# A new written order for the first twelve head pairs of a Longformer-attention and MLP kernel, with casting value loads and small transfers of the global value rows

## The chip, the core and the metric

The kernel runs on one core of a Trainium2 chip. A core has a matrix engine (TensorE, PE in the profile, with its weight loads as PEld), a vector engine (DVE), a scalar engine (ACT), a general engine (POOL) and a queue engine (SP). They run side by side, each through its own list of instructions in order, and wait for one another by semaphores. Transfers run on 16 shared DMA engines. Those issued by SP and ACT appear in the profile as the hardware queue, those issued by POOL as the software queue. TensorE writes its results to PSUM, where this kernel lays out eight banks of 128 x 512 fp32: three with the tag "s", two "h", one "o" and the two of `pv`.

The metric is the device time of one execution in microseconds, as the median of several runs. The profile is one execution recorded by the hardware profiler, and all times inside a run are read from it.

## What is computed

Attention over 8 batches of 8 heads (576 positions, 64 wide), with a band of 32 positions to each side and 8 global positions, and behind it an MLP over all 4608 tokens:

```python
scores = scale * np.matmul(q, k.transpose(0, 1, 3, 2))
mask = np.abs(pos[:, None] - pos[None, :]) <= window
mask = mask | is_global[:, None] | is_global[None, :]
scores = np.where(mask, scores, -1000000000.0)
...
attn = attn / (np.sum(attn, axis=-1, keepdims=True) + 1e-09)
return np.matmul(attn, v).astype(np.float32)
...
x = np.ascontiguousarray(attn_out.transpose(0, 2, 1, 3)).reshape(B * S, H * D)
h = x @ w_in
g = h * np.cos(h)
return (g @ w_out).astype(np.float32)
```

Inputs and output are fp32, `w_in` is 512 x 2048 and `w_out` 2048 x 512. The kernel computes in fp16 with fp32 sums.

## The kernel before

**Units of work.** Heads go in pairs, 32 of them (`pr`), four to a batch; two pairs are a half (`s`), which is also the unit in which k, q and v are loaded. A pair passes through these steps, each of which is one letter in a written order:

- `k` and `q` (`local_k`, `local_q`, lines 598 and 609): for pairs 0 to 9, TensorE turns the naturally laid-out rows (`turned`, line 588, 16 small transposes into one PSUM bank with the tag "h"), and ACT copies the bank to the buffers `kw` and `qb`. For pairs under `PK` = 4, 16 more small matmuls (`pick_globals`, line 307) pick the global columns out of the same rows; the other pairs get them from gathered rows through POOL copies (`g`, line 575). From pair 10 on the turning is done by DMA transposes, and DVE copies.
- `s` (`scores5`, line 621): ten matmuls `st` into three banks "s" and the one bank "o", four exponentials on ACT, three masked products `pm` on DVE.
- `p` (`values5`, line 641): 20 matmuls into `pv`, of which there is one buffer only, then on DVE the denominators and the product `xn` (line 666).
- `x` (`turn_x5`, line 670): five transposes into an "s" bank and DVE copies into `xT`, the input of the MLP. For the last pair of a batch eight POOL copies set the global columns.
- `n` (line 814): a square and sum of `xn` on ACT for a check of the value range.

Pairs 10 to 31 use a form with eleven blocks instead of five (lines 692 to 752).

**The MLP** is cut into units too. `1` is one block of `h` and its activation: four matmuls `ph` (line 762) for 512 tokens and 128 hidden columns, the cosine on ACT (line 768) and the product `g` on DVE (line 769). `2` is four of the 16 matmuls `po` (line 800) of one block of 128 output rows. A `1` for a block of tokens can only stand behind the batches that it covers (`ready`), and a `2` behind the `1`s that it needs. Cosine and exponential lie in different activation tables, so that each change from one to the other reloads a table (1283 ns in the profile).

**The order** is written by hand in strings of steps, and every engine executes its own instructions in that order. Behind a prologue (13 matmuls on ones, constants, masks, the first two turnings) stands `FRONT`: pairs 0 to 9 with no MLP unit before the step behind `x7`, in a rhythm of scores, turnings of the pair after, `x` and `p` of the pairs before, with 18 filling matmuls (`f`). Then `MID` has 26 of the units `1` and eight `2`, `FIFTH` has pairs 10 and 11 with two `1` and eight `2`, and from half 6 on `SIXTH` and then `ORDER` repeat: two pairs, eight `1` and eight `2` each. Behind the last pair the rest of the MLP runs alone.

**Loads.** POOL's queue brings k and q of a half by casting loads (`L`, line 279), the weights (`W` four times for `w_in`, `O` for `w_out`), and from half 5 on whole halves of v, k and q as fp16 into DRAM (`K`, line 268 to 272). For halves 0 to 4 the values come in fp32 by five transfers each on SP's queue (`M`, line 373), into a buffer that two halves share in turn, and a POOL cast (`C`, line 402) writes them as fp16 into the buffer `vw`, which `values5` reads. The eight global value rows of a half are then summed out of it by ten small matmuls and two ACT copies (`y`, line 404). From pair 10 on SP transposes k and q (`B`, line 284) and loads `vw` from DRAM, with the global rows `vg` copied in by two small transfers per pair (line 414). `V` and `U` are one-element POOL copies that hold back the `K` behind them until pair 10's q is there and pair 10's `xn` is done.

Of the kernel before, what the change touches and what calls it, by code (L numbers as in the profile page):

```python
# [9 lines left out]
FP32 = mybir.dt.float32  # L10
# [9 lines left out]
P = 128  # L20
NP = H // 2
# [7 lines left out]
PK = 4  # L29
# [18 lines left out]
ORDER = "sa 2 2 2 2 sz pa 1 1 2 xa pz G 1 1 2 xz n 1 1 2 kc qc 1 kd qd 2 1"  # L48
# [5 lines left out]
SIXTH = "sa 2 2 2 2 sz pa 1 1 2 xa pz G 1 1 2 xz n 1 1 D0 2 kc qc D1 1 kd qd D2 2 1"  # L54
# [150 lines left out]
def kernel(  # L205
# [44 lines left out]
    NN = 3  # L250
# [3 lines left out]
    qn = [keep.tile([QP, 2 * 2, RW, D], FP16, name=f"qn{i}") for i in range(2)]  # L254
    w_out16 = const.tile([P, NF, DM], FP16)
    kn.append(w_out16[0:KP, 0:4].rearrange("p h (r d) -> p h r d", d=D))
    qn.append(w_out16[0:QP, 4:8].rearrange("p h (r d) -> p h r d", d=D))
# [17 lines left out]
    def load_qk(s, hs=(0, 4)):  # L275

        base = (s * 4 + hs[0]) * S * D
        for src, dst in ((k, kn[s % NN][KPAD : KPAD + S // RW]), (q, qn[s % NN][0 : S // RW])):
            nc.gpsimd.dma_start(dst[:, hs[0] : hs[1]].rearrange("x h r d -> x h (r d)"),
                                dview(src, base, (RW * D, S // RW), (S * D, hs[1] - hs[0]), (1, RW * D)))  # L280
# [25 lines left out]

    def pick_globals(pr, t, src, ones, n, to):
# [5 lines left out]
        nc.scalar.copy(to, view(t, (0, to.shape[1]), (1, G)))  # L313
# [46 lines left out]
    vn32 = [work.tile([P, 4 * 2, 512], FP32, tag="g", name="vn32") for _ in range(2)]  # L360

    def vn_of(s):
        i = s if s < 4 else 2
        return view(vn32[i // 2][:, 4 * (i % 2)], (4 * D, NK5), (1, 4 * D))

    def load_vn(s, t0=0, t1=NK5):

        rows = vn_of(s)
        for t in range(t0, t1):
# [3 lines left out]
            nc.sync.dma_start(rows[p0 : p0 + n, t].rearrange("p (h d) -> p h d", h=4),  # L373
                              dview(v, (s * 4 * S + lo) * D, (D, n), (S * D, 4), (1, D)))

    def next_values(s):

        nc.vector.memset(vn_of(s)[0:64, 0], 0.0)
        load_vn(s)

    def clear_rows(s):

        nc.gpsimd.memset(vn_of(s)[0:G, 1:], 0.0)
# [11 lines left out]
    def vn16(s):  # L395
        return view(vw[s % NV], (4 * (D + 1), NK5), (D + 1, 4), (1, D + 1))

    def cast_vn(s):
        if s > 1:
            nc.gpsimd.tensor_copy(gate, pm_of[max(pm_of)][0:1, 2 * CN - 1 : 2 * CN])  # L400
        old, new = vn_of(s).rearrange("p t (h d) -> p t h d", h=4), vn16(s)
        nc.gpsimd.tensor_copy(new[:, :, :, 0:D], old)

    def value_rows(s, part):

        hs = slice(2 * part, 2 * part + 2)
# [493 lines left out]
    with tc.manual_schedule():  # L900
# [24 lines left out]
        for s in range(1, 4):  # L925
            clear_rows(s)
# [162 lines left out]
```

## Time and profile before

| | |
|---|---|
| median of 3 runs | 353.98 us (353.82 to 356.26) |
| profiled execution, its span | 353.2 us |
| PE busy | 332.5 us (94%) |
| DVE busy | 250.1 us (71%) |
| ACT busy | 245.9 us (70%) |
| POOL busy | 108.5 us (31%) |
| moved by DMA | 44.58 MB, mean 126 GB/s |
| chain that ended last | PE 73%, ACT 8%, DVE 5%, DMA 5% |

The profiled execution has no time of its own beside its span, so that the span stands for it: 353.2 us, 0.8 us under the median of the runs.

A row of a timeline gives the start in us, the busy time, the engine, the source line, the operation with what it writes and reads, and the count; in square brackets stands how long the engine was idle before it and what ended that. Instructions overlap in the engine's pipeline, so the cost of a group in a dense stretch is the distance from its start to the start of the next row rather than its busy time. A row of the stretch table gives the stretch, its length, the busy time and count for PE, PEld, DVE, ACT and POOL in this order, the granted TensorE clock (1.00 is full), the DMA share and GB/s.

### The profile page before, as it was taken

The page shows a single profiled execution, that of the slowest core. Times are in us where ns is not written, and L with a number is a line of the kernel's source. Part 1 is how long each engine was busy: PE and PEld are TensorE (multiplying, and loading weights), DVE is VectorE, ACT ScalarE, POOL GpSimd, SP SyncE. Part 2 cuts the span into 40 slices and gives each one's busy share as a digit, 9 for nine tenths or more (in the row PEclk, how much of TensorE's full clock was granted, in tenths as well). Part 3 has the DMA queues.
Part 4 walks back from the last instruction along what each step waited for, and adds up shares of the span by engine and source line. Part 5 has one row for each costly group of instructions (what it writes and reads, how often), then busy time and mean ns, then how long its engine had stood idle before and what let it go on. Part 6 is the DMA issues. An engine that isn't in the chain of part 4 may idle for free.

```text
span 353.2 us, 8389 instructions
## 1 busy us (share of the span) xinstructions
PE 332.5 (94%) x3169; PEld 170.9 (48%) x3169; DVE 250.1 (71%) x611; ACT 245.9 (70%) x423; POOL 108.5 (31%) x221
## 2 busy tenths in 40 slices
PE   7887789999986999999999999999999999999993
PEld 3566675444443444544444545454544444444442
DVE  6565888887586778778787979697878466556410
ACT  8778987884754877777878787777878856644300
POOL 8854847434070507050705071416000100000000
PEclk9898989999999999999999999999999999999998
DMA  5999993999999999999999999999980000100112
GB/s 82 186 149 165 167 192 41 207 164 132 165 147 160 146 199 135 178 118 194 143 187 139 183 139 176 135 161 153 179 93 32 31 32 30 60 32 30 58 63 68
DMA packets 165891, 44.58 MB, mean 126 GB/s; under 512 B 153764, under 2 KB 160996, under 8 KB 165668
## 3 DMA queue, kind: packets, MB, share of 16 engines
q1 hardware_dynamic: 105860, 26.70, 51.2%
q0 software_dynamic: 59984, 17.28, 50.5%
q8 instruction: 27, 0.44, 0.5%
q14 instruction: 20, 0.16, 0.2%
HBM read 44.41 MB, written 19.17 MB: 180 GB/s over the span
## 4 chain that ended last, share of the span: by engine, by line
PE 73%; ACT 8%; DVE 5%; DMA 5%; issue 4%; SPq 3%; POOL 1%; ACTq 0%; POOLq 0%; DVEq 0%
PE po L800 32%; PE ph L762 30%; PE tx L744 2%; DMA kn<-in_k_dram 2%; PE st L699 2%; ACT e L702 2%; PE pv L719 2%; ACT e L634 1%; DMA vw<-vg 1%; ACT e L707 1%; SPq L414 1%; PE po L782 1%; ACT e L638 1%; DVE xn L666 1%; DVE pm L639 1%
## 5 line engine op out<-in xcount | busy, mean ns | idle before, releaser
L762 PE MATMUL ph<-xT,w_in 128*128 128x512 f16 x576 | 140.3, 379 | 1.1 <-DVE g L769 0.3
L768 ACT ACTIVATE cos<-ph,pio 128x512 f16<-128x512 f32 x144 | 97.1, 687 | 62.1 <-PE ph L762 59.9
L800 PE MATMUL po<-w_out,g 128*128 128x512 f16 x560 | 135.4, 379 | 0.0
L769 DVE TENSOR_TENSOR g<-cos,ph 128x512 f16<-128x512 f16 x144 | 95.9, 685 | 42.9 <-ACT cos L768 41.7
L762 PEld LDWEIGHTS <-w_in 128*128 128x128 f16 x576 | 54.2, 97 | 64.6 <-issue 4.6
L800 PEld LDWEIGHTS <-g 128*128 128x128 f16 x560 | 53.7, 98 | 63.6
L703 DVE TENSOR_TENSOR pm<-e,mask 128x512 f16<-128x512 f16 x44 | 18.8, 426 | 19.0 <-ACT e L702 17.7
L702 ACT ACTIVATE e<-st 128x512 f16<-128x512 f32 x44 | 23.9, 594 | 10.0 <-PE st L699 9.8
L980 POOL COPY gate<-xn 1x1 f16<-1x1 f16 x8 | 1.4, 180 | 87.9 <-DVE xn L730 87.9
L752 POOL COPY xT<-xg 128x4 f16 x48 | 15.6, 325 | 32.5 <-DVE xT L747 29.9
L272 POOL DMA_DIRECT2D q<-in_q_dram x11 | 24.0, 2182 | 0.0
L818 ACT ACTIVATE xn<-xn 128x1536 f16<-128x1536 f16 (+1 forms) x16 | 22.5, 1407 | 0.0
L730 DVE TENSOR_TENSOR xn<-pv,r_all 128x768 f16<-128x768 f32 x22 | 21.1, 958 | 1.0
L805 ACT COPY o<-po 128x512 f32<-128x512 f32 x17 | 10.0, 586 | 14.7 <-PE po L800 14.3
L807 DVE COPY o<-po 128x512 f32<-128x512 f32 x18 | 12.4, 690 | 9.0 <-PE po L800 8.5
L272 POOL DMA_DIRECT2D k<-in_k_dram x11 | 18.1, 1645 | 0.9 <-issue 0.9
L768 ACT ACT_TABLE_LOAD x12 | 15.4, 1283 | 0.2
L719 PE MATMUL pv<-vw,pm 128*64 128x65 f16 x484 | 12.7, 197 | 2.7 <-DMA vw<-vg 2.7
L607 DVE COPY kw<-kT 128x1320 f16<-128x1320 f16 x22 | 15.1, 685 | 0.0
L702 ACT ACT_TABLE_LOAD x11 | 14.1, 1283 | 0.2
L699 PEld LDWEIGHTS <-kw 64*128 64x128 f16 x484 | 8.4, 95 | 10.7 <-issue 8.1
L699 PE MATMUL st<-qb,kw 64*128 64x64 f16 x484 | 11.2, 191 | 1.5 <-DVE qb L619 1.1
(185 smaller groups left out, 385.9 us busy)
## 6 DMA issues: line engine op xcount, KB each, us to landing
out_dram<-o SPq DMA_DIRECT2D x35, 256.0 KB
vw<-v SPq DMA_DIRECT2D x32, 165.0 KB
v<-in_v_dram POOLq DMA_DIRECT2D x11, 288.0 KB
k<-in_k_dram POOLq DMA_DIRECT2D x11, 288.0 KB
q<-in_q_dram POOLq DMA_DIRECT2D x11, 288.0 KB
vn<-in_v_dram SPq DMA_DIRECT2D x20, 120.0 KB
w_in<-in_moe_w_in_dram POOLq DMA_DIRECT2D x4, 512.0 KB
w_out<-in_moe_w_out_dram POOLq DMA_DIRECT2D x1, 2048.0 KB
```

The lines of the kernel that those rows point to most:

```text
L272: nc.gpsimd.dma_start(dst[s].rearrange("t (h d) -> t h d", h=4), dview(src, base, (D, S), (S * D, 4), (1, D)))
L699: nc.tensor.matmul(st[j // 8 * 2 + h][:, j % 8 * C : j % 8 * C + C], kp[hp, j], qp[hp, j], start=True, stop=True)
L702: nc.scalar.activation(e[:, 0:512], st[h], AF.Exp, scale=scale)
L703: nc.vector.tensor_tensor(view(pm[:, h], (1, 512)), e[:, 0:512], view(mask, (1, 512)), ALU.mult)
L719: nc.tensor.matmul(pv[r0 : r0 + C, j // 6, c0 : c0 + 65], pm[:, h, j], vp[:, j, h], start=True, stop=True)
L730: nc.vector.tensor_tensor(view(xn, (384, 2), (D, 6), (1, D)), view(pv, (512, 2), (65, 6), (1, D)), view(rp, (6, 2), (1, 6), (0, D)), ALU.mult)
L752: nc.gpsimd.tensor_copy(xT[:, :, bass.ds(pool_idx[g] + b * S, 1)], xg[:, :, g : g + 1])
L762: nc.tensor.matmul(ph, w_in16[:, j, f * P : (f + 1) * P], xT[:, j, t * TT : (t + 1) * TT], start=(j == 0), stop=(j == NC - 1))
L768: nc.scalar.activation(cos, ph, AF.Sin, bias=pio2)
L769: nc.vector.tensor_tensor(g, cos, ph, ALU.mult)
L800: nc.tensor.matmul(po, g16[:, f, s * P : (s + 1) * P], w_out16[:, f], start=(f == 0), stop=(f == NF - 1))
L818: nc.scalar.activation(view(xn, (BP * P, 2), (1, n)), view(xn, (BP * P, 2), (1, n)), AF.Square, accum_out=x_sq[:, s : s + 1])
```

## The change

`FRONT`, `MID` and `FIFTH` become one order, `OPENING`, in which the steps of pairs 0 to 11 stand in another sequence and the 32 `1` and 16 `2` stand among them. `:` lets the fourth bank of the scores be an "h" bank from there on, `R` sets `ready`, `X` is the POOL part of `x` as a step of its own. `PK` goes from 4 to 10, so that all of the first ten pairs pick their global columns by matmul. `ENGINES` says for each of these pairs which engine copies k, q, q's first columns and the picked columns (A is ACT, D is DVE). The filling matmuls and the holds `V` and `U` are no longer among the steps. The values of half 0 are loaded first of all, on SP's and ACT's queues, and are cast in two parts; those of halves 1 to 4 are cast by the load itself, in four transfers each on POOL's queue, straight into `vw`. The global value rows of half 0 still come by matmul (five, and two DVE copies), those of pairs 4 to 9 and of half 1 by two small SP transfers per pair from `vg16`, for which the gather of v comes early and its cast goes to DVE. k and q of halves 2 and 3 are loaded into a buffer of their own, `room`, and the rows around them are loaded too, instead of being cleared. The cosine takes its bias as a constant of the instruction. `B` stands inside the order as `T`.

```diff
-PK = 4
+PK = 10
...
+SIXTH = "sa 2 2 2 2 sz pa 1 1 2 xa pz G 1 1 2 xz n 1 1 D0 2 kc qc D1 1 kd qd D2 2 1 T"
+OPENING = ("s0 k1 q1 E2 k3 L2 L3 H2 I0 S4 k2 q2 C0.0 q3 C0.1 y0 s1 M1 k4 L4 p0 S5 s2 q4 q5 S2 p1 Z0 M2 s3 "
+           "S3 + k5 k7 p2 s5 q7 x0 W0 k6 p3 s4 W1 q9 S6 x2 x3 M3 q6 x1 p4 q8 S7 k8 W2 s7 k9 p5 s6 W3 "
+           "X0 O0 1 x4 1 : S8 1 K5 1 p6 M4 1 1 1 S9 n0 x5 1 p7 1 1 x6 1 Z1 E1 1 1 1 1 1 "
+           "- x7 1 2 s9 Z2 2 2 s8 n2 B5 2 + 2 X1 R2 E0 1 2 1 p8 n1 1 1 1 A2 p9 2 K6 Z3 "
+           "H0 Z4 2 B6 H1 g10 g11 1 Z5 q11 1 q10 g13 1 k10 1 K7 2 k11 2 s10 2 2 s11 p10 1 1 1 g12 - "
+           "x8 1 A1 2 p11 2 x9 k13 1 k12 x10 1 2 n4 q12 2 A0 x11 n3 R3 1 q13 B7")
+ENGINES = ("DAADAAAADD", "DAADADAAAA", "AAAADDDDAD", "AAAAAAAAAA")
...
-MID = ("+ 1 1 1 1 Z0 1 1 1 Z1 1 1 Z2 1 1 A0 n1 1 Z3 1 1 1 Z4 1 1 A1 n2 1 1 1 Z5 A2 1 1 1 n3 B5 1 2 2 g10 g11 kc qc V10 K6 2 2 1 1 2 2 kd qd - 2 2")
-FIFTH = "sa G 2 2 2 2 sz pa 1 1 2 xa U10 K7 pz 2 2 2 kc qc xz n kd qd"
-FRONT = ("M1 s0 E0 C0 E1 L2 k1 q1 w4 s1 y0.0 f4 k2 q2 C1 H0 p0 M2 L3 y0.1 s2 k3 q3 f2 x0 p1 M3 H1 g4 g5 g6 C2 y1.0 s3 g7 L4 I k4 q4 f2 x1 p2 M4 y1.1 s4 "
-         "C3 W0 k5 q5 f2 x2 p3 y2.0 s5 g8 g9 W1 W2 W3 k6 q6 f2 x3 p4 y2.1 s6 C4 Y0 k7 q7 f2 x4 p5 n0 y3.0 s7 k8 q8 f2 x5 p6 y3.1 s8 H2 k9 q9 f2 x6 p7 y4.0 s9 "
-         "x7 p8 y4.1 O m m x8 K5 p9 t t + m m t t x9 -")
...
+    vn32 = work.tile([P, 8 * 512], FP32, tag="g", name="vn32")
+    room = work.tile([P, NF, TT], FP16, tag="g", name="room")
...
+    for i in range(2):
+        kn.append(room[0:KP, 8 * i : 8 * i + 4].rearrange("p h (r d) -> p h r d", d=D))
+        qn.append(room[0:QP, 8 * i + 4 : 8 * i + 8].rearrange("p h (r d) -> p h r d", d=D))
...
+            queues[t].dma_start(rows[p0 : p0 + n, t].rearrange("p (h d) -> p h d", h=4),
+                                dview(v, lo * D, (D, n), (S * D, 4), (1, D)))
+    def load_vn(s, h0=0, h1=4):
+        for h in range(h0, h1):
+            nc.gpsimd.dma_start(vn16(s)[G:P, :, h, 0:D], dview(v, ((4 * s + h) * S - 24) * D, (D, KS), (KS * D, NK5), (1, D)))
...
-        nc.gpsimd.tensor_copy(new[:, :, :, 0:D], old)
+    def cast_vn(s, part):
+        hs = slice(2 * part, 2 * part + 2)
+        nc.gpsimd.tensor_copy(vn16(s)[:, :, hs, 0:D], vn_of(s).rearrange("p t (h d) -> p t h d", h=4)[:, :, hs])
...
+    def spread_vg(pr):
+        for h in range(2):
+            nc.sync.dma_start(vn16(pr // 2)[0:G, :, 2 * (pr % 2) + h, 0:D],
+                              view(vg16[pr * G : (pr + 1) * G, 0, h], (0, NK5), (1, D)))
...
-            nc.scalar.copy(k5(pr)[:, :, G:].rearrange("p n (j r) -> p n j r", r=RW),
+            COPY[ENGINES[0][pr]](k5(pr)[:, :, G:].rearrange("p n (j r) -> p n j r", r=RW),
...
-        tags = (("s", 3), ("s", 3), ("s", 3), ("o", 1))
+        tags = (("s", 3), ("s", 3), ("s", 3), ("o", 1) if front[0] else ("h", 2))
...
-        nc.scalar.activation(cos, ph, AF.Sin, bias=pio2)
+        nc.scalar.activation(cos, ph, AF.Sin, bias=pi / 2.0)
...
+        first_values((nc.sync, nc.scalar, nc.sync, nc.scalar, nc.sync))
...
-            gather((k, q)[x], (kg32, qg32)[x], 0)
+            gather((k, q, v)[x], (kg32, qg32, vg32)[x], 0)
```

More of the change, by code (lines that the diff above doesn't have):

```diff
@@ L358, in load_v, with vn16, first_values @@
                               dview(v16, lo + (QB * i0 - 32) * D, (D, W), (QB * D, i1 - i0), (1, D)))
-    vn32 = [work.tile([P, 4 * 2, 512], FP32, tag="g", name="vn32") for _ in range(2)]
     def vn_of(s):
[L363 to L369, printed above, removed]
+        return view(vn32, (4 * D, NK5), (1, 4 * D))
+    def vn16(s):
+        return view(vw[s % NV], (4 * (D + 1), NK5), (D + 1, 4), (1, D + 1))
+    def first_values(queues):
+        rows = vn_of(0)
+        for t in range(NK5):
             lo = max(KS * t - 24, 0)
@@ L668, in values5, with global_x @@
             view(rp, (NK5, 2), (1, NK5), (0, D)), ALU.mult)
+    def global_x(b):
+        xg = xg_of[b]
+        for g in range(G):
+            nc.gpsimd.tensor_copy(xT[:, :, bass.ds(pool_idx[g] + b * S, 1)], xg[:, :, g : g + 1])
     def turn_x5(pr):
@@ L923 @@
         index_rows(1)
-        load_vn(0)
-        for s in range(1, 4):
-            clear_rows(s)
         load_qk(1)
```

91 lines of the change are left out of this document (35 added, 56 removed), and 1 row of the table OPENING.

## The prediction

> **What bounds the kernel now.** I first cut the span at four places of PE's timeline: the first scores, the first MLP unit, the first scores of pair 12, where half 6 begins, and those of pair 14.
>
> ```profile
> 10.44 0.55 PE L631 MATMUL st<-qb,kw 64*128 64x136 f16 x10
> ...
> 41.48 0.55 PE L631 MATMUL st<-qb,kw 64*128 64x136 f16 x10 [0.16 <-ACT qb L616]
> ...
> 53.23 1.90 PE L762 MATMUL ph<-xT,w_in 128*128 128x512 f16 x8
> ...
> 102.18 0.67 PE L699 MATMUL st<-qb,kw 64*128 64x64 f16 x22 [1.12 <-DVE qb L619]
> ...
> 122.62 0.49 PE L699 MATMUL st<-qb,kw 64*128 64x64 f16 x22
> ...
> 139.76 0.49 PE L699 MATMUL st<-qb,kw 64*128 64x64 f16 x22
> ```
>
> The second row is pair 7's scores, the eighth of their kind. Then the stretch table by these cuts, and the same for line 762 and for line 800 alone:
>
> ```profile
> 10.40:53.20 42.80, 35.29 (x779) 27.69 (x778) 29.49 (x93) 35.76 (x84) 26.04 (x48) 0.88 1.06 171
> 53.20:102.20 49.00, 46.98 (x326) 22.27 (x326) 39.84 (x98) 34.17 (x53) 22.62 (x35) 1.00 1.21 143
> ...
> 122.60:353.20 230.60, 224.13 (x1819) 108.58 (x1818) 159.26 (x347) 152.90 (x246) 43.15 (x98) 1.00 0.95 113
> ```
> ```profile
> 53.20:102.20 49.00, 28.82 (x128) 12.22 (x128) 1.00 1.21 143
> ```
> ```profile
> 53.20:102.20 49.00, 14.65 (x64) 6.09 (x64) 1.00 1.21 143
> ```
>
> From 53.2 us on PE is the bound: 46.98 of 49.0 us, then 224.13 of 230.6. Before that no MLP unit runs, and the leading engine is ACT with 35.76 of 42.8 us (84%); PE's 35.29 there holds filling matmuls and matmuls at a clock of 0.88. So the kernel spends 43 us on ten pairs in which PE earns little, and the 32 + 16 units that follow (128 and 64 matmuls at four each) wait for them.
>
> **Part by part.** The change keeps the number of units ahead of half 6 (32 and 16 in both orders) and leaves `SIXTH` and `ORDER` as they were, so what is behind pair 14's scores, 353.2 - 122.62 = 230.6 us, is taken over. I work out when pair 14's scores start, in four stretches.
>
> *To the first scores.* Pair 0's two copies go to DVE, behind its mask building: one copy of this shape out of PSUM is 0.46 us below, so 0 to 0.9 us later; I take 0.4, start 10.8.
>
> *First scores to first unit.* The new order has eight `s`, six `p`, four `x` and the turnings of nine pairs ahead of its first `1`, where the old one had all ten pairs nearly done. Prices by distance of starts, PE, ACT, DVE:
>
> ```profile
> 20.00 0.55 PE L631 MATMUL st<-qb,kw 64*128 64x136 f16 x10
> 20.48 0.47 PE L595 MATMUL bank<-ident,kn 75*64 75x75 f16 x16
> 20.78 0.39 PE L312 MATMUL bank<-one_k,kn 75*64 75x8 f16 x16
> 21.03 0.45 PE L595 MATMUL bank<-ident,qn 76*64 76x76 f16 x16
> ...
> 21.81 0.44 PE L678 MATMUL tx<-ident,xn 128*128 128x128 f16 x5
> 22.09 1.03 PE L646 MATMUL pv<-vw,pm 128*128 128x65 f16 x20
> 23.05 0.28 PE L555 MATMUL t<-ident,g 128*128 128x128 f16 x2
> ```
> ```profile
> 38.52 1.01 ACT L634 ACTIVATE e<-st 128x488 f16<-128x488 f32 x2
> ...
> 40.19 0.63 ACT L604 COPY kw<-bank 128x600 f16<-128x600 f16 x1
> 40.73 0.15 ACT L615 COPY qb<-bank 128x8 f16<-128x8 f16 x1
> 40.78 0.64 ACT L616 COPY qb<-bank 128x600 f16<-128x600 f16 x1
> 41.33 1.26 ACT L818 ACTIVATE xn<-xn 128x1280 f16<-128x1280 f16 x1
> ```
> ```profile
> 36.00 0.72 DVE L635 TENSOR_TENSOR pm<-e,qT 128x488 f16<-128x488 f16 x2
> ...
> 37.11 0.46 DVE L679 COPY xT<-tx 128x600 f16<-128x600 f16 x1
> ...
> 37.66 0.14 DVE L660 TENSOR_REDUCE dg<-pv 8x2 f32<-8x8 f32 x1
> ...
> 38.19 0.83 DVE L666 TENSOR_TENSOR xn<-pv,r_all 128x640 f16<-128x640 f32 x1
> ```
>
> PE: scores 0.48, turning 0.30, picking 0.25, `x` 0.28, `p` 0.96. So 18 turnings with picks 9.9, seven `s` 3.4, six `p` 5.8, four `x` 1.1 and half 0's value rows some 0.8: 21.0 us. The picks of pairs 4 to 9 are added work, 12 x 0.25 = 3.0, which fits under the other engines. ACT: an exponential set 1.67, copies 0.54 and 0.55, a small copy 0.05: eight sets 13.4, 13 large copies 7.2 (the other five go to DVE), 22 small ones 1.1, so 21.7; the ACT copies of the value rows are gone. DVE: `pm` 1.11, `x` 0.55, `p` 37.66 to 39.02 = 1.36: eight `pm` 8.9, six `p` 8.2, four `x` 2.2, five large copies 2.3, the rest (value rows, a cast, small copies, part of a mask) an estimated 2.0, so 23.6. DVE leads now, narrowly. If the leading engine is busy to the 84% that ACT reached, the stretch takes 23.6 / 0.84 = 28.1 us: first unit at 38.9. Its bounds are a full DVE (34.4) and, as rival, the old rhythm.
>
> *First unit to pair 12.* This starts from the old 49.0 us and adds what moved behind the first unit:
>
> ```profile
> 72.26 1.88 DVE L769 TENSOR_TENSOR g<-cos,ph 128x512 f16<-128x512 f16 x3
> 75.90 3.20 ACT L768 ACTIVATE cos<-ph,pio 128x512 f16<-128x512 f32 x5
> ```
> ```profile
> L768 ACT ACT_TABLE_LOAD x12 | 15.4, 1283 | 0.2
> ```
>
> PE: 46.98 + three `p` 2.9 + four `x` 1.1 + two `s` 1.0 = 52.0. DVE: 39.84 + 4.1 + 2.2 + two `pm` 2.2 = 48.3. ACT: 34.17 + two sets 3.3 + one `n` 1.26 + two more table loads (exponentials of pairs 9 and 8 between cosines) 2.6 = 41.3. PE stays first. At the old density (46.98 / 49.0 = 0.959) it is 54.2 us, to 93.1. With DVE at 48.3 there is less slack than before, so some of it may be lost: a density of 0.90 gives 57.8. The cosine's constant bias I cost at nothing: no row shows that form, and even a fifth off the 0.63 us of each of 32 is 4 us of an engine with 13 us to spare in the stretch. The "h" bank for the scores takes a bank from the units only around pairs 8 and 9; 0 to 1 us, inside that density.
>
> *Half 6.* In the old order it took 20.44 us, where the next took 17.14. The chain of waits says why:
>
> ```profile
> 108.13 5.03 DMA vw<-vg
> ```
>
> Pair 12's and 13's values were late on SP's queue, behind a `K6` that `V` held until pair 10's q was ready. Now `K6` stands behind `p9` with no hold and `B6` some 25 us ahead of pair 12, so I take 17.14 + 0.5 for the two turnings of global rows that are peculiar to it: 17.6 (bounds 17.1 and 20.4). Pair 14 then starts at 110.7, and the span is 110.7 + 230.6 = 341.3 us.
>
> **Whether the loads keep up.** All wide loads and now the values of halves 1 to 4 stand in one line on POOL's queue. The last wide load that somebody waits for is `w_out`, at the first `2`: 16 units at (28.82 + 14.65) / 48 = 0.91, two `p`, four `x`, at 0.959, after 38.9, so at 57.1.
>
> ```profile
> 57.06 1.21 POOL L897 DMA_DIRECT2D w_out<-in_moe_w_out_dram  x1
> ...
> 72.59 0.95 POOL L335 DMA_INDIRECT vg<-in_v_dram,gidx_rows  x1 [5.29 <-DMA w_out<-in_moe_w_out_dram]
> 73.97 0.95 POOL L335 DMA_INDIRECT vg<-in_v_dram,gidx_rows  x1 [0.43 <-DMA v<-in_v_dram]
> ```
> ```profile
> 77.53 1.30 SPq L285 DMA_TRANSPOSE qT<-q  x1
> ```
> ```profile
> q0 software_dynamic: 4672, 0.88, 64.9%
> ```
> ```profile
> 29.72 3.16 DMA vn<-in_v_dram
> ```
> ```profile
> GB/s 82 186 149 165 167 192 41 207 164 132 165 147 160 146 199 135 178 118 194 143 187 139 183 139 176 135 161 153 179 93 32 31 32 30 60 32 30 58 63 68
> ```
>
> `w_out` (2048 KB) was issued by 58.27 and landed at 72.59: 14.3 us. Ahead of its end stand 5 x 576 KB of k and q, 2048 of `w_in` and its own 2048, 6976 KB: 48.7 us at that rate, 34.5 us at the best slice (207 GB/s), 41.6 between, as both have been seen. Half 0's values are 3.2 us. A casting value load has no row. Nearest is k and q of half 5, 4608 packets of the same 256 bytes in 73.97 to 77.53, so 2400 packets in 1.9 us; in a steady stretch of 17.1 us (132.5 to 149.6) the queue's 4672 packets took 64.9% of 16 engines, 38 ns each, so 2400 in 5.7. I take 1.9, since the line is not shared with a steady flow there. With three such loads and a start at about 5 us `w_out` lands at 5 + 41.6 + 3.2 + 5.7 = 55.5 (48.4 to 62.6), just in time; the upper end costs 5.5 us. The four POOL casts saved and the issues added about cancel on an engine that was busy 26.04 of 42.8 us. The first small transfers of value rows can come up to 2 us late for pair 2, if they land as late as the 5.03 us above; the rest are issued ahead.
>
> The Trainium skill, "DMA: Bandwidth & Descriptors", section Specifications, asks for 512 bytes or more per transfer for full rate, since less makes a read-modify-write. By that rule the 128-byte writes of the casting loads would fall behind the 256-byte fp32 loads that they replace; the rows above show the contrary (1.9 against 3.16 us), though into DRAM, and no row here shows it into a buffer.
>
> **Rivals.** *A, the old rhythm stays:* `p` of one pair waits for `xn` of the pair before in the single `pv` buffer, and eight scores took 41.48 - 10.44 = 31.0 us. Then the first unit comes at 42.3, and the time is 3.4 us more, or 6.2 with half 6 still at 20.4: spans of 344.7 to 347.5. For it: DVE did not lead and still the rhythm was slow. Against: the scores now run two and more pairs ahead of `p`.
>
> *B, slower, the software queue becomes the bound:* the wide loads go at 14.3 us per 2048 KB and each casting load takes 5.7 us. `w_out` lands at 62.6 + 3 x 3.8 = 74.0 instead of 57.1, PE stands still at the first `2`, and the span is 341.3 + 16.9 = 358.2. From 11.9 us of lateness on the kernel is slower than before. For it: DMA share 1.06 before the first unit. Against: the old fp32 loads took more time than these, and the wide ones were the same.
>
> ```profile
> 32.93 1.40 POOL L584 COPY qb<-qgT 128x32 f16<-128x32 f16 x1
> ```
>
> That row is a POOL copy of 32 columns that takes 1.40 us beside a busy DVE; were the 16 new issues stretched so, the queue would run dry and land there. The Trainium skill, "SBUF — State Buffer", section SBUF: two separate sides (the "DVE blocks DMA" trap), says that POOL cannot write descriptors while DVE holds the shared port in a two-port mode; by its figures (620 ns alone, 3100 beside a DVE copy) 16 issues would cost an estimated 40 us of POOL, and B would hold.
>
> **Numbers.** The profiled span is 0.8 under the median, so the forecast is 342.1 us. It has 0.57, with an own range of 336 (DVE full, density 0.98) to 347. A has 0.22 (345.5 to 348.3). B with its steps on the way has 0.21: about 0.03 still over 1% faster, 0.08 within 1%, 0.10 slower at about 359. A measurement of this kernel cannot tell less than about 1% (350.4 to 357.5) from no change. Faster: 0.57 + 0.21 + 0.03 = 0.81; within 1%: 0.09; slower: 0.10. The range of 336 to 354 leaves out some 0.05 below and 0.14 above.
>
> **What would show it.** First line-767 matmul at 36 to 41 us, first output matmul within a few us of 57, pair 12 at 90 to 97, the next half's scores about 17.6 later, and no wait of PE for `w_out` or `vw`. A first unit past 42 shows A. A PE idle time over 5 us ended by a DMA of `w_out`, `w_in` or `vw`, with POOL's value issues well over 0.8 us each, shows B. I am wrong as well if PE's density between the first unit and pair 12 falls under 0.88, which would mean that ACT's table loads and DVE's queue meet PE's units head on.

## The result, and the profile after

The changed kernel takes 356.05 us (median of 20 runs, 355.14 to 359.04), the kernel before 353.9 us (20 runs, 350.93 to 357.13); the ratio is 1.0088, with a 95% interval of 1.0065 to 1.011. The forecast was 342.1 us, with a range of 336 to 354. The profiled span is 354.0 us.

First the four cuts of the prediction, in TensorE's timeline of the changed kernel:

```profile
11.60 0.55 PE L634 MATMUL st<-qb,kw 64*128 64x136 f16 x10 [0.31 <-DVE qb L619]
...
52.38 1.89 PE L767 MATMUL ph<-xT,w_in 128*128 128x512 f16 x4
...
106.89 0.49 PE L705 MATMUL st<-qb,kw 64*128 64x64 f16 x22
...
124.39 0.49 PE L705 MATMUL st<-qb,kw 64*128 64x64 f16 x22
```

The stretches are 40.8, 54.5, 17.5 and 354.0 - 124.4 = 229.6 us. Forecast were 28.1, 54.2, 17.6 and 230.6. Three of four are right within 1 us; the whole error lies between the first scores and the first unit. The page's slices show what is different there (40 slices of 8.85 us; granted clock in tenths):

```profile
PE   7689999999899999999999999999999999999993
...
PEclk9955559999999999999999999999999999999998
```

In the slices three to six, 17.7 to 53.1 us, TensorE had half its clock; asked by half microseconds, from 17.1 to 54.6 us. The stretch table (columns as in the prediction), cut at the first `p`:

```profile
11.60:24.51 12.91, 8.31 (x250) 6.64 (x249) 5.69 (x17) 6.46 (x20) 8.27 (x12) 0.71 1.35 145
24.51:52.38 27.87, 27.48 (x556) 23.35 (x552) 19.73 (x65) 16.74 (x45) 17.46 (x26) 0.50 1.36 134
```

From the first `p` on TensorE is busy for 27.48 of 27.87 us at a clock of 0.50. DVE, which the forecast let lead, has 19.73. Ahead of the first `p` nobody is near full: DVE has 5.69 of 12.91 us. TensorE's timeline there:

```profile
15.87 0.39 PE L319 MATMUL bank<-one_k,kn 75*64 75x8 f16 x15
18.57 0.17 PE L319 MATMUL bank<-one_k,kn 75*64 75x8 f16 x1 [2.31 <-issue]
19.47 0.72 PE L598 MATMUL bank<-ident,qn 76*64 76x76 f16 x16 [0.73 <-DMA qn<-in_q_dram]
...
24.51 1.56 PE L649 MATMUL pv<-vw,pm 128*128 128x65 f16 x20
...
28.81 1.56 PE L649 MATMUL pv<-vw,pm 128*128 128x65 f16 x20
```

Three things are to be seen. TensorE stops in the middle of a pick, one matmul before its end, for 2.31 us for which the profile has no releaser ("issue"). Then it waits for the q of half 1. And behind these it runs at half clock: a `p` takes 1.56 instead of 1.03 us, and the distance from the first `p` to the second is 4.30 us.

### The profile page after: what moved, and what is told of

It reads as the page before. It is cut to its first block, busy times and chain, and to the rows that moved or that the text cites. A ratio compares the mean times of both kernels' runs of the same rounds, so it can differ in the third digit from the quotient of the medians.

```text
span 354.0 us, 8610 instructions
## 1 busy us (share of the span) xinstructions
PE 337.8 (95%) x3294; PEld 177.5 (50%) x3294; DVE 254.3 (72%) x622; ACT 223.7 (63%) x411; POOL 112.0 (32%) x213
## 4 chain that ended last, share of the span: by engine, by line
PE 82%; DMA 7%; ACT 5%; issue 2%; POOL 1%; SPq 1%; DVE 1%; ACTq 0%; POOLq 0%
PE ph L767 32%; PE po L805 32%; DMA qn<-in_q_dram 4%; PE pv L649 3%; DMA kT<-k 3%; PE bank L598 2%; PE tx L750 2%; PE st L705 2%; ACT e L708 2%; PE st L634 2%; PE bank L319 2%; PE pv L725 1%; ACT e L713 1%; PE tx L686 1%; PE po L787 1%
## 5 line engine op out<-in xcount | busy, mean ns | idle before, releaser
L767 PE MATMUL ph<-xT,w_in 128*128 128x512 f16 x576 | 142.8, 381 | 0.8 <-DVE g L774 0.2
L773 ACT ACTIVATE cos<-ph 128x512 f16<-128x512 f32 x144 | 84.4, 597 | 69.7 <-PE ph L767 62.6
L676 POOL COPY xT<-xg 128x4 f16 x64 | 18.9, 295 | 45.3 <-DVE xT L753 38.2
L823 ACT ACTIVATE xn<-xn 128x1536 f16<-128x1536 f16 (+1 forms) x16 | 22.6, 1415 | 0.0
L386 POOL DMA_DIRECT2D vw<-in_v_dram x16 | 15.3, 1102 | 7.6 <-DVE pm L638 4.2
L637 ACT ACTIVATE e<-st 128x488 f16<-128x488 f32 x20 | 10.5, 578 | 9.1 <-PE st L634 9.0
L610 DVE COPY kw<-kT 128x1320 f16<-128x1320 f16 x22 | 15.3, 694 | 0.1
```

Of the source, the lines that this page charges most:

```text
L386: nc.gpsimd.dma_start(vn16(s)[G:P, :, h, 0:D], dview(v, ((4 * s + h) * S - 24) * D, (D, KS), (KS * D, NK5), (1, D)))
L676: nc.gpsimd.tensor_copy(xT[:, :, bass.ds(pool_idx[g] + b * S, 1)], xg[:, :, g : g + 1])
L767: nc.tensor.matmul(ph, w_in16[:, j, f * P : (f + 1) * P], xT[:, j, t * TT : (t + 1) * TT], start=(j == 0), stop=(j == NC - 1))
L773: nc.scalar.activation(cos, ph, AF.Sin, bias=pi / 2.0)
L823: nc.scalar.activation(view(xn, (BP * P, 2), (1, n)), view(xn, (BP * P, 2), (1, n)), AF.Square, accum_out=x_sq[:, s : s + 1])
```

## The experiments

The first theories were: the clock alone (C, later the clock theory or the tensor-engine theory), and the loads together with rival A of the prediction, the chain from `p` to `xn` to the next `p` (D, later the chain theory). The kernels ran in six groups. Each group ran on one chip and is compared with the kernel before on that chip; the groups used five chips between them.

The first figure behind each expectation is the median, the second its ratio to the kernel before with the 95% interval.

**Fillings and a bridge.** Filling matmuls like the 18 of the old order put into the new one, 13 times four, and 14 wide matmuls of ones ahead of pair 2's q.

```diff
-... S4 k2 q2 C0.0 q3 C0.1 y0 s1 M1 k4 L4 p0 S5 s2 q4 q5 S2 p1 ...
+... S4 k2 w14 q2 C0.0 q3 C0.1 y0 f4 s1 M1 k4 L4 f4 p0 S5 s2 q4 f4 q5 S2 f4 p1 ...
...
-... + k5 k7 p2 s5 q7 x0 W0 k6 p3 ...
+... + k5 f4 k7 f4 p2 s5 q7 f4 x0 W0 k6 f4 p3 ...
```

> The changed kernel with 14 full matmuls on ones ahead of the turning of pair 2's q (where PE stood still for 3 us) and with four filling matmuls (128 x 184 each) at 13 places up to the first MLP unit. Theory C (the granted clock fell to 0.50 at that standstill and stayed there for 37.5 us, because the small matmuls of this order do not raise it again): the clock stays at or returns to 1.00 for most of the stretch, the first MLP unit comes at 42 to 46 us instead of 52.4, and the time is 6 to 10 us under the changed kernel. Rival D (the loads and the chain of p and xn set the stretch, the clock only follows): first unit still at 52 or later, since the added matmuls cost 4 us of PE, and the time is the changed kernel's or up to 4 us more.

355.93 us, ratio 1.0071 (1.0034 to 1.0109); first unit at 53.25. Its stretch table from the scores of pair 1 on, and one row of its waits there (us in total, times, longest):

```profile
26.10:53.25 27.15, 24.22 (x644) 20.88 (x643) 21.27 (x67) 17.90 (x47) 18.12 (x27) 0.93 1.28 137
```
```profile
PE pv L496 <- DVE xn L669: 2.7, 5, 0.8
```

The clock is back (0.93 in the mean, 1.00 from 22 to 49 us) and the first unit is not earlier. That looked like the end of theory C. But the fillings write the `pv` tile, and the second row shows what they do there: five of them wait for `xn`, in front of whatever follows. TensorE's 24.2 us of 27.15 hold the fillings too, and the 14 wide ones, at half clock, had put pair 1's scores off from 22.6 to 26.1 us. What the clock gained was given back.

The two parts by themselves, with the same steps:

> The changed kernel with the 14 full matmuls alone, no filling ones. If the fall of the clock comes from the standstill alone, the clock is 1.00 through the stretch and the first unit comes at 38 to 42 us. If it comes from the low activity of turnings and picks, the clock falls to 0.50 within one or two of its windows of 3.4 us behind the burst and stays there, and the first unit comes within 3 us of 52. By rival D (loads), no change of the time beyond 1 us either way.

358.43 us, 1.0124 (1.0071 to 1.0178); the clock was 1.00 from 24.7 to 35.0 us and fell again without fillings; first unit at 54.72. In the ten microseconds at full clock, with no filling matmul in between, the second `p` follows the first after 3.12 us, where the changed kernel has 4.30:

```profile
28.69 1.03 PE L649 MATMUL pv<-vw,pm 128*128 128x65 f16 x20 [0.29 <-DVE vw L408]
...
31.81 1.03 PE L649 MATMUL pv<-vw,pm 128*128 128x65 f16 x20 [0.45 <-DVE xn L669]
```

> The changed kernel with the filling matmuls at the 13 places, without the 14 full ones. If fillings are enough to raise the clock again, it falls at about 17 us, is back at 1.00 before 28 us, and the first unit comes at 43 to 48. If not, the clock stays at 0.50 to the first unit, and with 8 us of fillings at half clock that comes at 56 to 60 us.

357.38 us, 1.0136 (1.0058 to 1.0214); the clock was 1.00 from 28.8 to 49.3 us, so the fillings do raise it; first unit at 51.93, a miss for the 43 to 48 that this was to give.

**The kernel before without its fillings** (`w4`, `f4` and all `f2` out of `FRONT`; beside the four wide ones that are 18 fillings and not the 22 of the expectation).

> The kernel before without its four warm and 22 filling matmuls between the pairs. Theory C: windows at 0.50 get more than the three of before and join up, the first MLP unit comes 2 to 10 us later than 53.2, and the time is 2 to 8 us over before. Rival D: the same time as before or up to 2 us less, since 5 us of PE work is gone.

355.51 us, 1.0039 (1.0002 to 1.0076). The scores of pair 2 and of pair 3 in it, at half clock, and those of pair 3 in the kernel before, where pair 2's stand at 20.00 and the clock between them is full:

```profile
20.28 0.91 PE L631 MATMUL st<-qb,kw 64*128 64x136 f16 x10
...
26.07 0.29 PE L631 MATMUL st<-qb,kw 64*128 64x136 f16 x1
```
```profile
23.82 0.22 PE L631 MATMUL st<-qb,kw 64*128 64x136 f16 x1
```

From pair 2 to pair 3 it is 5.79 us instead of 3.82, so the pair takes 2.0 us more where the clock is down. Without the fillings the clock was 0.50 from 14.0 to 34.0 us; with them it fell as well, but only for about 3.4 us at a time. Still the first unit comes only 0.9 us later than in the kernel before, at 54.09, a miss for theory C's 2 to 10 us. Most of what the half clock cost in the first pairs does not reach the first unit there; why is not shown.

**What the stretch waits for.** Three edits of the changed kernel. The scores of pair 1 ahead of the turnings of pairs 2 and 3:

```diff
-s0 k1 q1 E2 k3 L2 L3 H2 I0 S4 k2 q2 C0.0 q3 C0.1 y0 s1 M1 ...
+s0 k1 q1 s1 E2 k3 L2 L3 H2 I0 S4 k2 q2 C0.0 q3 C0.1 y0 M1 ...
```

> Changed kernel with the scores of pair 1 moved from behind the turnings of pairs 2 and 3 to right behind those of pair 1. Start theory (everything is late because pair 1's scores stand behind turnings whose k and q land only at 15.0 and 19.4 us): scores of pair 1 at 14 to 15 instead of 22.6, first unit at 45 to 48 instead of 52.4, time about 350. Tensor-engine theory (behind 22 us TensorE at half clock is the bound, 29.39 of 29.78 us busy): only the 0.9 us of that one step is gone, first unit at 51 to 52.4, time within 1.5 us of the changed kernel's 356. Chain theory (p waits xn of the pair before): first unit at 49 to 52.

361.07 us, 1.019 (1.0135 to 1.0245). Pair 1's scores start at 15.97, the first `p` still at 25.25, the first unit at 53.15. From the first `p` to the first unit that is 27.90 us, as in the changed kernel (27.87). The scores were not what the start waited for. The first unit is 0.8 us past the range of the tensor-engine theory, and the time is 5 us longer than that theory allows; most of that stands behind the first unit and is taken up below.

Picks of pairs 4 to 9 with one of their eight steps over `r`:

```diff
-        for r in range(RW):
+        N = RW if pr < 4 else 1
+        for r in range(N):
```

> Changed kernel in which the picks of pairs 4 to 9 run 2 of their 16 matmuls, so the global columns of those pairs' k and q are left incomplete. Tensor-engine theory: 12 picks times 14/16 of 0.52 us at half clock is 5.5 us less on the bound, first unit at 46 to 48, time about 351. Chain theory: the picks lie beside the chain, first unit at 51.4 to 52.9, time within 1.5 us of 356.

358.59 us, 1.008 (1.0034 to 1.0125); first unit at 50.35, 2.0 us earlier. The direction is TensorE's, the size is not: 46 to 48 was expected. At 40.77 TensorE now waits 1.55 us for half 4's q, and its standstill in pair 2's pick was 2.95 us here.

Fillings of 104 columns into free columns of the turning's own bank, four ahead of each turning from pair 2 on:

```diff
+        for _ in range(BF if pr > 1 else 0):
+            nc.tensor.matmul(bank[:, 408:512], ones16, ones16[:, 0:104], start=True, stop=True, skip_group_check=True)
         for r in range(RW):
```

> Changed kernel with four filling matmuls of 104 columns ahead of each turning from pair 2 on, written to free columns of the turning's own bank, so that no filling waits for xn and none delays p by a wait (0.17 us each at full clock, 2.7 us in all). Tensor-engine theory (half clock is what makes TensorE the bound, and the fillings of the earlier runs only failed to show it because they waited in the pv chain): granted clock 1.00 from about 22 to 26 us on, first unit at 44 to 48, time about 350. Chain theory (VectorE and the pv buffer set the period, whatever the clock): clock 1.00 and the first unit still at 50 to 53, time 354 to 357. If the clock stays at 0.50 the run tells nothing of it, and the first unit comes 2 to 5 us later.

366.61 us, 1.0343 (1.0288 to 1.0399); first unit at 59.68.

```profile
21.00:59.60 38.60, 38.28 (x713) 31.53 (x707) 22.18 (x68) 19.78 (x53) 21.61 (x32) 0.50 1.14 124
```

These fillings did not raise the clock, and the first unit came about 7 us later: TensorE at half clock is full (38.28 of 38.60 us), so every matmul added to it is paid. That is the bound which the changed kernel has.

**The leading fillings.** Two, then four fillings directly ahead of each of the first six `p`, where TensorE waits for `xn` in any case, and six wide matmuls ahead of pair 3's k and of pair 2's q (`E2 w6 k3`, `k2 w6 q2`, `f2 p0` to `f2 p5`; then `f4`).

> Changed kernel with six wide matmuls of ones ahead of pair 3's and of pair 2's turnings (into the wait for k and q of half 1) and two filling matmuls directly ahead of each of the first six p, where PE waits for xn in any case. Clock theory (TensorE at half clock is the bound of the stretch before the first unit): if the granted clock is 1.00 from 26 us on, TensorE has some 22 us of work there, the period from pair to pair is 3.4 to 3.7 us, first unit at 45 to 48, time 347 to 351. Chain theory (p to xn to the next p, VectorE in order): at the same clock the period stays at 4.1, first unit at 51 to 53, time 353 to 356. If the clock falls all the same, the six and six wide matmuls add 1 to 3 us and the run tells nothing of the chain.

> The same with four filling matmuls ahead of each p. Clock theory: as with two, first unit at 46 to 49, if the clock is 1.00 there; chain theory: 51 to 53. That the number of fillings decides over the clock: here it is 1.00 from 26 us on, and with two it is not.

With two 363.09 us, 1.0196 (1.0128 to 1.0264): the clock fell at 21 us and stayed; first unit at 56.10. With four 362.69 us, 1.0192 (1.0118 to 1.0266): the clock was 1.00 from about 37 to 50 us, and not from 26 us on as expected; first unit at 55.02. In the second's timeline:

```profile
20.14 0.33 PE L319 MATMUL bank<-one_k,kn 75*64 75x8 f16 x7 [3.56 <-issue]
...
37.72 1.03 PE L649 MATMUL pv<-vw,pm 128*128 128x65 f16 x20
...
41.13 1.03 PE L649 MATMUL pv<-vw,pm 128*128 128x65 f16 x20
...
51.16 0.59 PE L598 MATMUL bank<-ident,kn 75*64 75x75 f16 x12 [2.26 <-issue]
```

Two readings. At full clock and without a wait in between, `p` follows `p` after 3.41 us, so the chain by itself is no slower than that. And there are standstills without a releaser, in which the clock falls here. Where the first stands was counted, by the stretch table from 0 to a time within it, in the changed kernel, in the run with pair 1's scores early and in this one:

```profile
0.00:18.40 18.40, 11.81 (x222) 6.42 (x223) 11.76 (x54) 7.40 (x18) 13.19 (x27) 0.96 1.02 133
```
```profile
0.00:19.00 19.00, 12.73 (x222) 7.34 (x223) 12.69 (x56) 9.10 (x22) 13.92 (x28) 0.94 1.05 133
```
```profile
0.00:18.50 18.50, 12.65 (x222) 6.82 (x223) 11.55 (x54) 7.40 (x18) 13.32 (x27) 1.00 1.05 131
```

It is behind the 222nd matmul each time, whatever stands at that place (a trace can miss single matmuls). So it belongs to the stream of instructions, not to a tile. The list of DMA queues has one named "instruction", with packets of 16 KB; asked by half microseconds it shows one such packet between 15.5 and 16.0 us in the changed kernel, some 2.6 to 3.1 us before TensorE goes on at 18.57. In the run with four leading fillings the packet is moved between 17.0 and 17.5 us, and TensorE goes on at 20.14. The packet of the changed kernel:

```profile
q8 instruction: 1, 0.02, 14.6%
```

**Fewer loads ahead of that packet.** The k and q of halves 2 and 3 issued behind the casts of half 0's values; and the same with four leading fillings.

```diff
-... k3 L2 L3 H2 I0 S4 k2 q2 C0.0 q3 C0.1 y0 s1 M1 ...
+... k3 H2 I0 S4 k2 q2 C0.0 q3 C0.1 L2 y0 s1 L3 M1 ...
```

> Changed kernel with the k and q loads of halves 2 and 3 issued only behind POOL's casts of half 0's values (at about 19 instead of 10.1 us), so that half 1's loads and the 16 KB packet of TensorE's instructions have less ahead of them. In all runs of the new order so far TensorE stood still behind its 222nd matmul without a wait, until 18.6 to 20.3 us. Supply theory (the packet is late because the loads crowd it): the packet is moved at 13 to 14 instead of 15 to 17 us, the standstill is under 0.7 us, half 1's q lands before 17.5, and the clock stays at 1.00 past 20 us unless pair 4's k, now issued 9 us later, is late itself; first unit at 46 to 51. If the loads have nothing to do with it: standstill of 1.2 to 3.5 us at the same matmul, first unit at 52 to 56.

361.19 us, 1.0174 (1.0107 to 1.0241); first unit at 51.80. The packet is moved between 13.0 and 13.5 us, and the standstill is gone:

```profile
16.73 0.63 PE L319 MATMUL bank<-one_k,kn 75*64 75x8 f16 x16
19.35 0.72 PE L598 MATMUL bank<-ident,qn 76*64 76x76 f16 x16 [1.99 <-DMA qn<-in_q_dram]
```

But half 1's q lands no earlier (19.3 and not before 17.5), TensorE waits for it instead, and the clock falls all the same. That the standstill comes from the crowd of loads is shown: none of the five runs with the two loads moved has it. That it makes the clock fall is not. In this run the clock fell at 15.2 us, in a wait of 1.21 us ahead of pair 3's k, and in the first three variants and the one with shortened picks it fell between 14.5 and 15.2 us, in the same wait (1.2 to 1.8 us) and ahead of the standstill.

> The same with four filling matmuls directly ahead of each of the first six p. Clock theory: where the granted clock is 1.00, the distance from p to p is 3.4 to 3.7 us, as it was between 37.7 and 41.1 us of the run with four leading fillings, and 4.5 to 5 where it is 0.50; with the clock held from pair 1 on the first unit comes at 45 to 48 and the time is 347 to 351. Chain theory: 4.1 at either clock, first unit at 50 to 53.

360.91 us, 1.0158 (1.009 to 1.0226); first unit at 52.22. The clock was not held from pair 1 on, but it was 1.00 from about 28 to 41 us:

```profile
28.95 1.03 PE L649 MATMUL pv<-vw,pm 128*128 128x65 f16 x20
...
32.82 1.03 PE L649 MATMUL pv<-vw,pm 128*128 128x65 f16 x20
...
36.23 1.03 PE L649 MATMUL pv<-vw,pm 128*128 128x65 f16 x20
...
40.34 0.47 PE L598 MATMUL bank<-ident,qn 76*64 76x76 f16 x16 [2.50 <-DMA qn<-in_q_dram]
```

3.87 and 3.41 us at full clock, where theory C expected 3.4 to 3.7 and the chain theory 4.1. Then half 4's q is late, which the slow TensorE of the changed kernel hides.

**The wait for half 1's q filled as well.** Eight wide matmuls ahead of pair 2's q in addition (`k2 w8 q2`), which fill the wait; and in a second kernel pair 9's q behind the `p` of pair 4 (`p4 q9 q8`).

> The late loads and the four leading fillings, with eight wide matmuls of ones ahead of pair 2's q, into the 2.0 to 2.5 us for which PE waits for half 1's q there. Clock theory: clock 1.00 from the first scores to about 36 us, first p at 22 to 24, p to p 3.4 to 3.9 us, then a wait of some 2.5 us for half 4's q at pair 9's turning, first unit at 45 to 48 instead of 52.4, time 347 to 352. Chain theory: first unit at 50 to 53 at full clock. If the clock falls before 20 us in spite of the eight, first unit at 51 to 54 and nothing is told.

360.5 us, 1.0208 (1.0149 to 1.0266). The profiled execution was the shortest of four, 356.29 us:

```profile
25.85 1.03 PE L649 MATMUL pv<-vw,pm 128*128 128x65 f16 x20
...
29.29 1.03 PE L649 MATMUL pv<-vw,pm 128*128 128x65 f16 x20
...
33.41 1.03 PE L649 MATMUL pv<-vw,pm 128*128 128x65 f16 x20
...
36.82 1.03 PE L649 MATMUL pv<-vw,pm 128*128 128x65 f16 x20
...
39.96 0.47 PE L598 MATMUL bank<-ident,qn 76*64 76x76 f16 x16 [1.62 <-ACT e L641]
...
47.48 0.82 PE L767 MATMUL ph<-xT,w_in 128*128 128x512 f16 x3
```
```profile
13.35:25.85 12.50, 11.86 (x262) 8.41 (x262) 5.29 (x11) 6.17 (x20) 7.13 (x8) 0.64 1.23 143
25.85:47.48 21.63, 18.65 (x574) 16.33 (x572) 18.76 (x62) 16.52 (x45) 13.62 (x22) 1.00 1.30 134
```

The clock was not held from the first scores on: it fell at 8.7 us, and the eight wide matmuls brought it back at 22.2 us. The expectation gave 51 to 54 for a clock that falls before 20 us; the first unit came at 47.48 all the same, since from the first `p` on the clock was full. From there to the first unit it is 21.63 us, where the changed kernel has 27.87 at half clock: 6.2 us less, with the fillings in it and a wait of 1.62 us that ends with half 4's q and with an exponential alike. DVE leads by a hair, 18.76 us or 87% to TensorE's 18.65; the forecast had taken 84% for the whole stretch. The first unit is in the range of theory C and below that of the chain. The median did not follow; below.

> The same with the turning of pair 9's q behind the p of pair 4, so that the wait for half 4's q does not stand ahead of that p. Clock theory: 1 to 3 us earlier than the run before it, first unit at 43 to 46, and the time under the kernel before's by 1 to 2.5%. Chain theory: first unit at 50 to 53.

360.05 us, 1.0179 (1.0121 to 1.0237); first unit at 49.97. A miss: the `p` ahead of which q had stood came earlier (40.80), but then TensorE waited for half 2's values and for ACT, and the clock fell at 45.5 us.

**What becomes of the earlier first unit.** In the bridged run, the one before this, pair 10's scores are 4.4 us earlier than in the changed kernel (87.83 against 92.27), pair 12's are not (107.44 against 106.89). TensorE stands in pair 10's `p` in pieces. So the changed kernel itself was run again, beside one in which three units stand ahead of that `p` (`s11 1 1 1 p10 g12`).

> The changed kernel itself once more, beside the next one. In the last nine variants of it PE stood in the middle of pair 10's p in four or five pieces, 2.0 to 4.2 us in all, which the first profile of it and the first three variants don't show. If that depends on where it runs, it may show here too, and then the time is 358 to 362, the distance from pair 10's to pair 12's scores 19 instead of 14.6 us; if it comes from the edits, that distance is 14.6 and the time 355 to 357. First unit at 52 to 54 in both, with the standstill behind the 222nd matmul and a clock of 0.50 up to 52.

360.15 us, 1.0145 (1.0113 to 1.0178). First unit at 52.67, and 19.8 us from pair 10's to pair 12's scores instead of 14.6. TensorE in pair 10's `p`, then ACT beside it:

```profile
95.98 0.42 PE L725 MATMUL pv<-vw,pm 128*64 128x65 f16 x6
96.88 0.19 PE L725 MATMUL pv<-vw,pm 128*64 128x65 f16 x1 [0.47 <-issue]
97.59 0.22 PE L725 MATMUL pv<-vw,pm 128*64 128x65 f16 x2 [0.52 <-issue]
...
99.00 0.40 PE L725 MATMUL pv<-vw,pm 128*64 128x65 f16 x12 [0.53 <-issue]
```
```profile
99.14 1.08 ACT L708 ACTIVATE e<-st 128x512 f16<-128x512 f32 x2 [3.18 <-remote]
```

So it is not made by the edits: from the run with pair 1's scores early on, every profile of the new order had it, the changed kernel's too, and the first profile of the changed kernel and the first three variants did not. Where it stands the change costs 1.45%, not 0.88%.

It also hid what the earlier first unit is worth. The scores of pair 12, in the bridged run and in this second profile of the changed kernel, which both have the standstill:

```profile
107.44 0.49 PE L705 MATMUL st<-qb,kw 64*128 64x64 f16 x22
```
```profile
112.45 0.49 PE L705 MATMUL st<-qb,kw 64*128 64x64 f16 x22
```

The bridged run is 5.2 us ahead at the first unit (47.48 against 52.67), 5.0 at pair 12 and 5.1 in the span (354.6 against 359.7). So the time that the clock gave was not lost behind it, in this one execution. The other three of that kernel took 359.39 to 362.50 us at a mean clock of 0.95 to 0.96 instead of 0.974, and its median is no shorter than the changed kernel's 360.15.

> The bridged, late-loaded order with leading fillings, in which pair 10's p stands behind the three units that followed it. First unit at 46 to 48.5 (clock theory, as in the run with the bridge; the chain theory's 50 to 53 has fallen there). If what pair 10's p stands for arrives at a time of its own, the units cover it: pair 10's to pair 12's scores 15 to 17 us, pair 12's at 103 to 105, time 350 to 353. If it is a matter of that p's place in the instruction stream, it stands there as before, pair 12's at 106.5 to 108.5, time 355 to 360.

362.73 us, 1.0218 (1.0186 to 1.0251); first unit at 54.56, since the clock fell at 27 us behind a wait of 1.40 us for half 2's q. Pair 10's `p` is in one piece there, but a unit ahead of it stands 2.77 us, and ACT 3.20 us in front of pair 11's exponentials as before; 19.7 us up to pair 12's scores. So the p's place in the order is not what it hangs on, and the units did not cover it. What stops several engines together at that place is open.

**Parts of the change in the kernel before.** The hold ahead of half 6's cast taken out (`V10`), the cosine's bias as a constant, and both.

```diff
-... g10 g11 kc qc V10 K6 2 2 ...
+... g10 g11 kc qc K6 2 2 ...
...
-        nc.scalar.activation(cos, ph, AF.Sin, bias=pio2)
+        nc.scalar.activation(cos, ph, AF.Sin, bias=pi / 2.0)
```

> Kernel before without the hold ahead of half 6's cast, nothing else changed. If that hold is what made half 6 take 20.4 us, half 6 takes 17.3 to 17.8 and the time is about 351 (ratio 0.992). If half 6 was slow for another cause (its place in the order, the units around it), it stays at 20 and the time within 1 us of 354.

354.18 us, 0.9964 (0.9922 to 1.0005); no difference beyond the interval. Half 6 took 18.1 us in its one profile, an execution of 359.72 us.

> Kernel before with the cosine's constant bias alone. ScalarE's 144 cosines cost 597 instead of 687 ns each (13 us of ScalarE's busy time in all); ScalarE does not set the end behind the first unit, so the time stays within 1 us of the kernel before. If ScalarE were near the bound there, it would be 2 to 5 us less.

353.41 us, 0.9935 (0.9893 to 0.9977). The cosine's group in the kernel before and in this one:

```profile
L768 ACT ACTIVATE cos<-ph,pio 128x512 f16<-128x512 f32 x144 | 97.1, 687 | 62.1 <-PE ph L762 59.9
```
```profile
L768 ACT ACTIVATE cos<-ph 128x512 f16<-128x512 f32 x144 | 84.2, 596 | 70.2 <-PE ph L762 62.4
```

The 13 us of ACT are there, most of them as idle time. The median is 2.2 us lower, a little more than "within 1 us"; where in the span it comes from, the one profile doesn't tell, since its rest behind pair 14's scores is 230.7 us as in the kernel before.

> Kernel before with the two parts that cost nothing there: the constant bias of the cosine, and no hold ahead of half 6's cast. Half 6 takes 17.3 to 18.2 instead of 20.4 us; together 2 to 4 us less, ratio 0.988 to 0.995. If the clock's falls decide more than both, the ratio's interval holds 1.

352.34 us, 0.9919 (0.9883 to 0.9955): the quickest of all, ahead of both kernels. Half 6 in it, and in the kernel with the constant alone, which still has the hold:

```profile
103.73 0.67 PE L699 MATMUL st<-qb,kw 64*128 64x64 f16 x22 [0.83 <-DVE qb L619]
...
122.17 0.49 PE L699 MATMUL st<-qb,kw 64*128 64x64 f16 x22
```
```profile
103.03 0.67 PE L699 MATMUL st<-qb,kw 64*128 64x64 f16 x22 [1.11 <-DVE qb L619]
...
121.42 0.49 PE L699 MATMUL st<-qb,kw 64*128 64x64 f16 x22
```

18.4 us both, so the hold by itself is worth nothing that these profiles show. What the first profile of the kernel before had, with its 20.44 us, is two waits of TensorE for the small transfers of global value rows:

```profile
108.43 0.64 PE L719 MATMUL pv<-vw,pm 128*64 128x65 f16 x22 [1.59 <-DMA vw<-vg]
...
113.20 0.74 PE L719 MATMUL pv<-vw,pm 128*64 128x65 f16 x22 [1.10 <-DMA vw<-vg]
```

These 2.7 us are 0.2 to 0.6 in the four other profiles of the old order, with the hold and without it.

The changed kernel has both parts, the constant bias and no hold. So the rest of it costs more than the 0.88%: by the two ratios some 1.7% (1.0088 / 0.9919), an estimate that takes the parts to add up.

## Why the prediction was wrong

- **To the first scores:** forecast 10.8, measured 11.60, in its bounds.
- **First scores to first unit: the step that failed.** It put TensorE at 21.0 us of work, from rows at full clock, and let DVE lead with 23.6 at 84%. DVE's sum was near (5.69 + 19.73 = 25.4 us). TensorE's was 35.8 us (8.31 + 27.48), because the clock was 0.50 from 17.1 us on, and from the first `p` on it was the bound. The prediction had read the old stretch's clock of 0.88 and its fillings; it had the changed kernel without the fillings, said that the picks' 3.0 us "fits under the other engines", and nowhere asked what clock the new stretch would get. With the clock at 1.00, the same work from the first `p` on took 21.6 us instead of 27.9, in one execution, with DVE and TensorE level.
- The other part of it is the start. The 84% was laid over the whole stretch, but the first `p` stands behind the turnings of pairs 2 and 3, whose k and q land at 15 and 19.4 us: 12.9 us from the first scores to the first `p`, where the kernel before has 18.74 - 10.44 = 8.3. What this start takes at full clock no run shows: it was 12.5 us at a mean clock of 0.64 in the bridged run and 11.5 at 0.85 in the last one of the new order. So of the 12.7 us over the forecast some 6.2 are the clock behind the first `p`. The largest known piece of the rest is the start's 4.6 us over the kernel before (12.9 - 8.3). This division is a reckoning; no run took both away. That moving half 0's value rows and the first `p` ahead of those turnings would gain the start was not tried.
- **First unit to pair 12** (54.2, measured 54.5), **half 6** (17.6, measured 17.5) and the rest (230.6, measured 229.6) were right in size in the first profile; in the second, with the standstill in pair 10's `p`, the first of these was 59.8. (The order has four `1` behind `Z1 E1`, not the five printed in its diff, so the count of 32 stands.) For half 6 the late value rows were read rightly, 2.7 us of waits in the profile from which the forecast was made. The reason given for them, the hold, is not borne out: with the hold and the old order, the kernels without fillings (122.51 - 104.15) and with the constant bias took 18.4 us. So the 17.6 came out right without its reason. Why the rows were late in that one profile stays open.
- **Loads:** no wait of TensorE for `w_out`. The first `2` starts at 70.72 and not 57, since all is later. In the first profile no wait for the small value rows shows either. The casting loads cost POOL 1102 ns each instead of some 0.8 us, 15.3 us for the sixteen of halves 1 to 4 and not the estimated 40; the software queue did not become the bound by that. But crowding was not harmless: it delayed TensorE's own instructions, and half 4's q stands next in line at full clock.
- **Rival A** was too early as well with its first unit at 42.3, and its sign, a first unit past 42, was too wide: it came, but not by the chain, since `p` to `p` is 3.1 to 4.1 us at full clock where no load is late, and 4.3 and more at half in the changed kernel. **Rival B** did not happen. That TensorE at half clock would be the bound was none of the rivals.

The Trainium skill, "TensorE: Matmul & The Clock Gate", section Part 1: The HAM clock gate, says that the clock comes back after one busy window of about 3.4 us. Taken as time in which the profile has TensorE busy, the rows above disagree for this mix of matmuls, of which about a third are transposes: 27.48 of 27.87 us busy at 0.50, and 38.28 of 38.60 with fillings of 104 columns. In these runs wide matmuls brought it back, MLP units, 14 or 8 of 512 columns, or groups of four with 184, and not always at once. Which of the small matmuls keep it down was not tried one by one.

## What to carry to other kernels

When an edit takes filling matmuls out, or sets small matmuls in a row with a wait among them, price TensorE at half clock as a case of its own, and look whether it becomes the bound. Lay a density only over a stretch whose inputs are there; time the first product of a chain from the landing of what it waits for. If fillings are put in, put them where TensorE waits anyway, since a filling that writes a shared tile brings a wait of its own. That fillings pay in this order is not shown: no kernel that had them was clearly faster than the changed kernel.

## What the hardware did that was not expected

- The clock stayed at 0.50 from 17.1 to 54.6 us, and from 17.6 to 55.1 us in the second profile of the same kernel, though TensorE was busy for 27.48 of 27.87 us from the first `p` to the first unit.
- TensorE stood behind its 222nd matmul for 1.2 to 3.6 us in the new order until two loads ahead of the 16 KB packet of instructions were moved behind it.
- The cosine with a constant bias takes 596 ns instead of 687 for 128x512.
- In the new order's later profiles, on four chips, ACT stands for 3 to 4 us in front of pair 11's exponentials while TensorE stands in pieces; in the three on a fifth chip and in the first profile neither does. Whether the chip decides it is not shown, and the cause stays open.
